# Seven GpSimd instructions fewer, and another order of VectorE's last products, in a state-space block with a gated FFN

## The chip, the cores and the metric

The kernel runs on one core of a Trainium2 chip. The metric is the device time of one execution in microseconds (us); a run gives one time and, for the core, its span in the profile's records. The time is usually 2.1 to 2.4 us longer than the span. In about one run of eight it is 2.8 to 3.9 us longer while the span is as usual, so spans are given beside times where tenths matter.

## The reference

Input x has 2048 tokens of 512 channels. It is normalised, then goes through two branches:

```python
xn = layernorm(x)
# branch A: a diagonal complex recurrence over the 2048 tokens
Bu = xn @ B_bar.T                       # complex, 512 states
h_t = Lam_bar * h_{t-1} + Bu_t
s = 2 * Re(h @ C.T) + xn * Dskip
# branch B: gated FFN with 1376 hidden columns, then silu
g = silu((gelu(xn @ w_gate) * (xn @ w_up)) @ w_down)
out = x + s * g
```

## The kernel before

The tokens are cut into four slabs (s = 0 to 3) of 512. TensorE does per slab: 11 pairs of products with w_gate and w_up (`g_ps`, `up_ps`, tile j), the input products of the recurrence (`u_ps`), the down projection (`f_ps`, four blocks of 11 matmuls) and the output product of the recurrence (`y_ps`). ScalarE applies gelu and copies (`gt`, `ub`). VectorE multiplies the two (`at`), rotates the states (`pp`, `qq`, `Wt`, `hst`), runs the scans (`Ft`) and multiplies and adds the outputs (`yg`, `ot`).

VectorE executes in program order, and the Python that writes the program decides that order with estimated clocks and a list of waiting work. An entry of the list is put in front of a new instruction when it would end by the time the new one is ready plus a tolerance `late`:

```python
def drain(t, late):
    while waiting and max(clk["dve"], waiting[0][0]) + waiting[0][1] <= t + late:
        pop()                                   # emits the head of the list

def dve(ready, cost, f, late=0.8):
    drain(ready, late)
    clk["dve"] = max(clk["dve"], ready) + cost
    f()                                         # emits the new instruction

def ffn(s, j, at):
    ...                                         # matmuls, gelu, copy
    if j == NFT - 1:                            # last tile, 96 rows
        dve(now() + lag, 0.36, lambda: TT(out=at[:fs, j, :], in0=gt[:fs, 0, :], in1=ub[:fs, 0, :], op=ALU.mult))
    elif i:                                     # two tiles at once
        dve(now() + lag, 0.63, lambda: TT(out=at[:, j - 1 : j + 1, :], in0=gt[:], in1=ub[:], op=ALU.mult))
```

The x of slab 3 is loaded late, since slab 0 keeps other data in its place until then; ScalarE takes its sums (`junk`), VectorE finishes the statistics (`ln_small`):

```python
def load_x(s):
    nc.sync.dma_start(out=x_tok[:, s * M : (s + 1) * M, :], in_=x_r[:, s * M : (s + 1) * M, :])
...
    if s == 1:
        load_x(3)
    for m in range(M):
        g2s[s, m] = down(s, m, ats[s])
        ...
        if s == 1:
            ln_act(3, m)
    if s == 1:
        ln_small(3)
```

## Time and profile before

| | before |
|---|---|
| times of the first three runs | 183.33, 183.81, 183.12 us |
| span in the profile | 181.0 us |
| TensorE busy | 96% of the span |
| VectorE busy | 89% |
| ScalarE busy | 62% |
| GpSimd busy | 12%, 49 instructions |

### The profile page before, as it was taken

What the parts mean: (1) busy time and instruction counts of PE and PEld (TensorE: products, weight loads), DVE (VectorE), ACT (ScalarE), POOL (GpSimd) and SP (SyncE); (2) the same over time, 40 slices, a digit from 0 to 9 for tenths busy, and PEclk for the clock granted to TensorE, in tenths of its full rate; (3) what the DMA queues carried; (4) which work ended last, traced back from release to release, by engine and by line L of the source; (5) the groups of instructions that cost most, each with busy time, mean ns of one, the idle gap of its engine ahead of it and who ended that gap; (6) DMA issues with size and microseconds to landing.
All of it is one profiled execution on the core that took longest, in us unless ns stands there. A gap on an engine that the chain in (4) does not pass through costs nothing.

```text
span 181.0 us, 2421 instructions
## 1 busy us (share of the span) xinstructions
PE 174.4 (96%) x842; PEld 82.9 (46%) x858; DVE 162.0 (89%) x256; ACT 112.4 (62%) x198; POOL 21.7 (12%) x49
## 2 busy tenths in 40 slices
PE   7899999999999999999999999999999999989992
PEld 2684444444444444444444444444444444444451
DVE  4789999997979999999958999999999999999163
ACT  3599766777699983681399953367239454563500
POOL 3795416004100000000004000000000000000000
PEclk9999999999999999999999999999999999999999
DMA  5999597961002300001300002510000000000011
GB/s 146 306 332 177 116 246 179 278 93 29 0 0 50 66 4 29 29 0 60 114 4 0 0 0 70 130 38 0 2 0 0 7 27 29 29 29 0 0 54 62
DMA packets 25644, 12.37 MB, mean 68 GB/s; under 512 B 15809, under 2 KB 25633, under 8 KB 25633
## 3 DMA queue, kind: packets, MB, share of 16 engines
q1 hardware_dynamic: 25456, 12.16, 28.3%
q8 instruction: 6, 0.10, 0.3%
q10 hardware_dynamic: 176, 0.07, 0.1%
q14 instruction: 6, 0.04, 0.1%
HBM read 6.46 MB, written 2.10 MB: 47 GB/s over the span
## 4 chain that ended last, share of the span: by engine, by line
DVE 44%; PE 42%; issue 5%; ACT 4%; DMA 3%; another core or an unknown queue 0%; SPq 0%; DVEq 0%; ACTq 0%
DVE Ft L432 12%; PE up_ps L243 10%; PE g_ps L243 10%; PE f_ps L493 9%; PE u_ps L385 8%; DVE qq L402 6%; DVE yg L526 5%; DVE pp L402 4%; PE y_ps L513 4%; DVE hst L406 4%; DMA x_tok<-in_A_x_dram 3%; DVE at L486 3%; DVE ot L527 3%; DVE Wt L406 3%; ACT junk L558 2%
## 5 line engine op out<-in xcount | busy, mean ns | idle before, releaser
L243 PE MATMUL g_ps<-xnT,wg 128*128 128x512 bf16 (+3 forms) x196 | 45.3, 353 | 0.5 <-DVE xnT L203 0.2
L243 PE MATMUL up_ps<-xnT,wu 128*128 128x512 bf16 (+3 forms) x188 | 45.2, 361 | 0.2
L493 PE MATMUL f_ps<-wd,at 128*128 128x512 bf16 (+1 forms) x172 | 38.7, 379 | 0.8 <-DVE at L484 0.6
L477 ACT ACTIVATE gt<-g_ps 128x512 bf16<-128x512 f32 (+1 forms) x44 | 27.1, 616 | 17.8 <-PE g_ps L243 16.1
L478 ACT ACTIVATE ub<-up_ps 128x512 bf16<-128x512 f32 (+1 forms) x44 | 27.0, 613 | 5.6 <-PE up_ps L243 5.0
L432 DVE TENSOR_TENSOR_SCAN Ft<-rho,it,Wt 128x512 bf16<-128x512 f32 x24 | 29.5, 1270 | 0.0
L385 PE MATMUL u_ps<-xnT,BT 128*128 128x512 bf16 x125 | 28.3, 379 | 0.2
L243 PEld LDWEIGHTS <-wg 128*128 128x128 bf16 (+1 forms) x200 | 19.1, 100 | 19.5 <-issue 0.5
L513 PE MATMUL y_ps<-C,hst 128*128 128x512 bf16 x119 | 27.6, 379 | 0.1
L243 PEld LDWEIGHTS <-wu 128*128 128x128 bf16 (+1 forms) x192 | 18.8, 100 | 19.1
L493 PEld LDWEIGHTS <-at 128*128 128x128 bf16 (+1 forms) x176 | 17.1, 98 | 21.7 <-DVE at L484 1.1
L390 ACT ACTIVATE U<-u_ps 128x512 bf16<-128x512 f32 x32 | 19.1, 597 | 9.8 <-PE u_ps L385 9.7
L498 ACT ACTIVATE g<-f_ps 128x512 f32<-128x512 f32 x16 | 9.5, 593 | 17.5 <-PE f_ps L493 17.5
L385 PEld LDWEIGHTS <-BT 128*128 128x128 bf16 x128 | 12.5, 98 | 15.1 <-DMA BT<-in_A_B_re_dram 0.2
L513 PEld LDWEIGHTS <-hst 128*128 128x128 bf16 x120 | 11.8, 98 | 14.1
L526 DVE TENSOR_TENSOR yg<-y_ps,g 128x512 bf16<-128x512 f32 x15 | 10.2, 682 | 5.8 <-PE y_ps L513 5.3
L486 DVE TENSOR_TENSOR at<-gt,ub 128x1024 bf16<-128x1024 bf16 x20 | 13.6, 679 | 0.0
L406 DVE TENSOR_TENSOR hst<-pp,qq 128x1024 bf16<-128x1024 bf16 x16 | 10.7, 688 | 0.3
L406 DVE TENSOR_TENSOR Wt<-pp,qq 128x1024 bf16<-128x1024 bf16 x16 | 10.4, 689 | 0.2
L402 DVE TENSOR_TENSOR pp<-U,cos_b 128x2048 bf16<-128x2048 bf16 x8 | 9.7, 1218 | 0.1
L402 DVE TENSOR_TENSOR pp<-Ft,cos_b 128x2048 bf16<-128x2048 bf16 x8 | 9.8, 1219 | 0.1
L402 DVE TENSOR_TENSOR qq<-U,sin_b 128x2048 bf16<-128x2048 bf16 x8 | 9.7, 1218 | 0.0
(116 smaller groups left out, 144.0 us busy)
## 6 DMA issues: line engine op xcount, KB each, us to landing
out_dram<-ot SPq DMA_DIRECT2D x15, 128.0 KB, 1.7
x_tok<-in_A_x_dram SPq DMA_DIRECT2D x3, 512.0 KB, 7.1
wd<-in_B_w_down_dram SPq DMA_DIRECT2D x1, 1280.0 KB
wg<-in_B_w_gate_dram SPq DMA_DIRECT2D x2, 256.0 KB, 4.3
wu<-in_B_w_up_dram SPq DMA_DIRECT2D x2, 256.0 KB
wg<-in_B_w_gate_dram SPq DMA_DIRECT2D x1, 512.0 KB, 6.5
wu<-in_B_w_up_dram SPq DMA_DIRECT2D x1, 512.0 KB
wg<-in_B_w_gate_dram SPq DMA_DIRECT2D x1, 352.0 KB
```

What stands on the lines that cost most here:

```text
L243: nc.tensor.matmul(ps[:fs, a:b], lhsT=w[:, kt, fsl], rhs=xnT[:, kt, s * TS + a : s * TS + b], start=(kt == 0), stop=(kt == KT - 1),)
L385: nc.tensor.matmul(u_ps[:, :], lhsT=BT[:, ri, kt, pt * P : (pt + 1) * P], rhs=xnT[:, kt, cols], start=(kt == 0), stop=(kt == KT - 1),)
L390: ACT(out=U[:, ri, q, :], in_=u_ps[:, :], func=AF.Copy)
L402: TT(out=box[key][:], in0=src()[:], in1=tab[:, hs, :].unsqueeze(1).to_broadcast(W), op=ALU.mult)
L406: return lambda: TT(out=dst()[i], in0=box["pp"][:, i, :, :], in1=box["qq"][:, 1 - i, :, :], op=op)
L432: nc.vector.tensor_tensor_scan(out=box["F"][:, ri, q, :], data0=rho[:, pt : pt + 1].to_broadcast([P, TS]), data1=box["W"][:, ri, q, :], in ...
L477: ACT(out=gt[:fs, i, :], in_=g_ps[:fs, :], func=AF.Gelu_apprx_tanh)
L478: ACT(out=ub[:fs, i, :], in_=u_ps[:fs, :], func=AF.Copy)
L486: dve(now() + lag, 0.63, lambda: TT(out=at[:, j - 1 : j + 1, :], in0=gt[:], in1=ub[:], op=ALU.mult))
L493: nc.tensor.matmul(f_ps[:, :], lhsT=at[:fs, k, m0 : m0 + P], rhs=wd[:fs, k, :], start=(k == 0), stop=(k == NFT - 1))
L513: nc.tensor.matmul(y_ps[:, :], lhsT=hst[:, j // NPT, j % NPT, m0 : m0 + P], rhs=C2[:, j // NPT, j % NPT, :], start=False, stop=(j == 2 * N ...
L526: TT(out=yg[:], in0=y_ps[:, :], in1=g2[:], op=ALU.mult)
```

## The change

The intent: take work off GpSimd (the identity is built in bf16 at once, three constants are set on VectorE, a factor 2 goes into a denominator, a bias that slab 1 does not use is not computed), move work into VectorE's waits, and put the last gate products of slab 3 ahead of waiting scans. The core of the diff (cuts marked):

```diff
-    ident_f = consts.tile([P, P], FP32, name="ident_f")
-    make_identity(nc, ident_f[:])
     ident = consts.tile([P, P], BF16, name="ident")
-    nc.gpsimd.tensor_copy(out=ident[:], in_=ident_f[:])
+    make_identity(nc, ident[:])
-    nc.gpsimd.memset(mhalf[:], -0.5)          # likewise eps, euler
+    nc.vector.memset(mhalf[:], -0.5)
...
+        GS(out=den[:], in0=den[:], scalar1=0.5, scalar2=None, op0=ALU.mult)
-        GS(out=cre[:], in0=cre[:], scalar1=2.0, scalar2=None, op0=ALU.mult)
-        GS(out=cim[:], in0=cim[:], scalar1=2.0, scalar2=None, op0=ALU.mult)
...
-        dve(now() + 0.8, 0.66, lambda: STT(   # fold_c, first half
+        dve(now() + 1.7, 0.7, lambda: STT(
-        dve(now() + 1.6, 0.66, lambda: STT(   # fold_c, second half
+        dve(now() + 2.4, 0.7, lambda: STT(
...
-            dve(now() + lag, 0.36, lambda: TT(...))
+            dve(now() + lag, 0.36, lambda: TT(...), 0.0 if s == NS - 1 else 0.8)
-            dve(now() + lag, 0.63, lambda: TT(...))
+            dve(now() + lag, 0.65, lambda: TT(...), 0.0 if s == NS - 1 and j > 8 else 0.8)
...
-        dve(now() + 1.0, 0.3, f)              # ln_small
+        dve(now() + 3.0, 0.3, f)
...
+        if x == 2:                            # nb only for slab 2
             G.tensor_tensor(out=nb[:, x, :], in0=mv[:, x, :, 0], in1=rs[:, x, :], op=ALU.mult)
             G.tensor_scalar(out=nb[:, x, :], in0=nb[:, x, :], scalar1=-1.0, scalar2=None, op0=ALU.mult)
```

More of the change, by code (lines that the diff above doesn't have):

```diff
@@ L140 @@
     eps = consts.tile([P, 1], FP32, name="eps")
-    nc.gpsimd.memset(eps[:], EPS)
+    nc.vector.memset(eps[:], EPS)
     sd = consts.tile([P, M], FP32, name="sd")
     euler = consts.tile([P, NPT], FP32, name="euler")
-    nc.gpsimd.memset(euler[:], math.e)
+    nc.vector.memset(euler[:], math.e)
     def small(name, w=NPT):
@@ L483, in ffn @@
         if j == NFT - 1:
-            dve(now() + lag, 0.36, lambda: TT(out=at[:fs, j, :], in0=gt[:fs, 0, :], in1=ub[:fs, 0, :], op=ALU.mult))
+            dve(
+                now() + lag, 0.36,
+                lambda: TT(out=at[:fs, j, :], in0=gt[:fs, 0, :], in1=ub[:fs, 0, :], op=ALU.mult),
+                0.0 if s == NS - 1 else 0.8,
+            )
         elif i:
-            dve(now() + lag, 0.63, lambda: TT(out=at[:, j - 1 : j + 1, :], in0=gt[:], in1=ub[:], op=ALU.mult))
+            dve(
+                now() + lag, 0.65, lambda: TT(out=at[:, j - 1 : j + 1, :], in0=gt[:], in1=ub[:], op=ALU.mult),
+                0.0 if s == NS - 1 and j > 8 else 0.8,
+            )
     def down(s, m, at):
@@ L623, in ln_vector_small @@
         G.tensor_tensor(out=rs[:, x, :], in0=vx[:, x, :], in1=mhalf[:], op=ALU.pow)
-        G.tensor_tensor(out=nb[:, x, :], in0=mv[:, x, :, 0], in1=rs[:, x, :], op=ALU.mult)
-        G.tensor_scalar(out=nb[:, x, :], in0=nb[:, x, :], scalar1=-1.0, scalar2=None, op0=ALU.mult)
+        if x == 2:
+            G.tensor_tensor(out=nb[:, x, :], in0=mv[:, x, :, 0], in1=rs[:, x, :], op=ALU.mult)
+            G.tensor_scalar(out=nb[:, x, :], in0=nb[:, x, :], scalar1=-1.0, scalar2=None, op0=ALU.mult)
     vx = consts.tile([P, NS, M], FP32, name="vx")
```

## The prediction

> **What bounds the kernel now.** I read the page first (busy shares, slices), then the waits of TensorE, then the VectorE and TensorE timelines, and last the neighbourhood of the one late wait.
>
> ```profile
> PE 174.4 (96%) x842; PEld 82.9 (46%) x858; DVE 162.0 (89%) x256; ACT 112.4 (62%) x198; POOL 21.7 (12%) x49
> PE f_ps L493 <- DVE at L484: 0.6, 1, 0.6
> PE tp L181 <- DVE xn L171: 0.2, 1, 0.2
> PE g_ps L243 <- DVE xnT L203: 0.2, 1, 0.2
> ```
>
> The first line gives busy us per engine, the others who TensorE (PE) waited for (total, times, longest). TensorE is busy for 96% of the span; after its first real matmul at 6.4 us it records one wait, 0.6 us, for the last gate product of slab 3 (line 484). GpSimd (POOL) is busy 12% and nowhere in that list. So the time is TensorE's stream plus a head and a tail, and only what shortens one of these three shows in the time.
>
> The late wait in the timeline (start, duration, engine, line, operation):
>
> ```profile
> 158.42 2.45 DVE L432 TENSOR_TENSOR_SCAN Ft<-rho,it,Wt 128x512 bf16<-128x512 f32 x2
> 160.37 0.59 ACT L478 ACTIVATE ub<-up_ps 96x512 bf16<-96x512 f32 x1 [0.33 <-PE up_ps L243]
> 160.79 0.67 DVE L486 TENSOR_TENSOR at<-gt,ub 128x1024 bf16<-128x1024 bf16 x1
> 161.38 1.28 DVE L432 TENSOR_TENSOR_SCAN Ft<-rho,it,Wt 128x512 bf16<-128x512 f32 x1
> 162.57 0.40 DVE L484 TENSOR_TENSOR at<-gt,ub 96x512 bf16<-96x512 bf16 x1
> ```
>
> VectorE runs a scan at 161.38 although the input of the last product was ready at 160.37 + 0.59 = 160.96. The product ends at 162.97, and TensorE resumes at 163.02. Three of the four down-projection blocks, and what follows the last one:
>
> ```profile
> 40.06 9.68 PE L493 MATMUL f_ps<-wd,at 128*128 128x512 bf16 x43
> 82.38 9.68 PE L493 MATMUL f_ps<-wd,at 128*128 128x512 bf16 x43
> 160.11 2.32 PE L493 MATMUL f_ps<-wd,at 128*128 128x512 bf16 x10
> 163.02 7.53 PE L493 MATMUL f_ps<-wd,at 96*128 96x512 bf16 x33 [0.59 <-DVE at L484]
> 170.39 5.13 PE L513 MATMUL y_ps<-C,hst 128*128 128x512 bf16 x23
> ```
>
> The next group after the first block starts at 49.57, after the second at 91.89: both 9.51 us from first matmul to next group (44 matmuls, 0.216 each). The last block takes 170.39 - 160.11 = 10.28. So the real loss is 10.28 - 9.51 = **0.77 us**; the 0.59 shown is less because the modelled end of a matmul overlaps the gap.
>
> **What the Trainium skill says.** "Perfetto Trace Analysis", Optimization Strategies: when the matmul engine is idle waiting for others, optimize the engines on the critical path. The trace agrees: all 21.7 us of GpSimd work leave no wait on TensorE. The same page, Tensor Engine Instruction, says ScalarE, VectorE and GpSimd are strict FIFO: an instruction put early in the list also blocks everything behind it. The trace agrees with the cost of that: VectorE stood still 1.82 us for the statistics at line 564. "SBUF — State Buffer", Who interferes with whom: a VectorE instruction with two SBUF inputs contends with GpSimd instructions that read SBUF. Here it is GpSimd that varies (the product of line 624 takes 0.20 us at 20.27 and 0.59 at 44.52), while VectorE's line 402 takes 1.20 and 1.22 beside busy GpSimd (26.4 to 28.7) and 1.22 without. So removing GpSimd work should give VectorE little.
>
> **Part 1, the start (identity, constants).** Removed on GpSimd: the cast of line 130, 0.29 us, and three memsets of 0.10. Identity is complete at about 1.64 and first used at 4.70, behind eight warm-up matmuls; eps is complete at 2.23 and first used at 4.51 behind the statistics. The head hangs on x landing at 2.80, then VectorE and ScalarE. The three memsets added to VectorE cost about 0.06 each (the one of line 126) in a gap from 1.12 to 2.80. **Effect 0.**
>
> **Part 2, coefficients and slab 1 and 2 statistics.** One halving of den is added (about 0.2 us, the tiny operations of lines 306 to 313), two doublings go (0.22 + 0.62), and two operations on nb for slab 1 go (0.20 + 0.24). The coefficient chain ends at 30.17 now and at about 29.3 then; it is first used at 43.1. The slab 1 norm needs rs, not nb. **Effect 0.**
>
> **Part 3, order on VectorE.** The kernel fixes this order with two clocks and a waiting list. I followed that rule on paper with old and new constants; with the old ones it gives the sequence in the timeline. Three groups move.
>
> - Folding of C (43 to 53 us). Two z products now fill part of the 1.06 us wait (0.7), and qq fills the 0.88 us wait before the last fold. Then the first gate product of slab 1, which needs ScalarE's ub at 54.16 + 0.62 = 54.78, makes VectorE wait some 0.6. Net VectorE gain about 0.35; TensorE sees none of it, as it has no wait there.
> - Slab 3 statistics (93 to 100 us). A pp of 1.14 (start to start) goes into the 1.82 us wait. But the product of slab 2, tiles 0 and 1, now precedes the second hst. It needs ub, done at 98.51 + 0.62 = 99.13, while VectorE would reach it at about 97.9. So the 1.14 gained is given back in a 1.2 us wait; hst would end near 100.4, where product after hst ended about 100.3 before: **0 to 0.15 later**, no gain. From here to 167.9 VectorE had no gap, so nothing else gives it time.
> - End of slab 3. New order: scan 0, products 8 and 9, product 10, scans 1, 2, 3. Step by step: scan 0 at 158.42 as before, products 8 and 9 at 159.65 (their ub was ready at 158.58 + 0.60 = 159.18), finished issuing at 160.25. Then VectorE waits, head of line, for ub at 160.96: about 0.75 us idle. Product 10 runs 161.02 to 161.42. TensorE reaches the eleventh matmul of the block at 160.11 + 10 x 0.216 = 162.27. Margin 0.8 us, so the wait is **gone, -0.77 us**.
>
> What the idle 0.75 costs: scan 1 at 161.34, scans 1.19 apart, pp 1.31 after the last one's start at 163.72, thus 165.03; qq 166.17; hst 167.42 to 168.71 instead of 167.88, 168.86 with the slab 2 delay. The y matmuls will start at 170.39 - 0.77 = 169.62, and their third is the first to need this half. Margin over 0.7. After that the tail is TensorE-paced (VectorE waits for y_ps 4.5, 0.57, 0.58 us), so it moves whole.
>
> Sum: 0 + 0 + 0 - 0.77. Span 181.00 - 0.77 = 180.23; time 183.33 - 0.77 = **182.56 us**, 0.4% less.
>
> **Rivals.** (a) The wait moves from at to hst: VectorE idles 0.75, and the last scan chain is 0.8 to 1.0 later. For it: VectorE has no gap between 96 and 167.9, so any delay travels to the end. Against it: before, hst was done 2.5 us ahead of the y matmuls. It needs a further delay of 0.8; then the gain shrinks from 0.77 to between 0 and 0.5: 182.8 to 183.3. (b) GpSimd matters for the head: the seven instructions shorten the start, or the freed read port speeds VectorE. For it: VectorE did wait 0.43 us for s2a at 10.82. Against it: that chain begins at 5.26, on pf from ScalarE, and none of its links is removed. At best 0.2 to 0.4 more: 182.2. (c) The earlier placement of gate products or y products makes VectorE late in slabs 1 to 3 until TensorE lacks a buffer or hst. Against it: checked at each moved y product, its matmuls are done before VectorE arrives (slab 3, block 1: 146.46 against 146.83, the closest). If it happened, 0.5 to 1 us: 183.3 to 184.
>
> **Range and chances.** The three runs before spread over 183.12 to 183.81, so a median moves by 0.2 to 0.3 on its own. Centre 182.6; rival (b) and luck give 182.2, rival (a) and ill luck 183.2. A change of 2% would be 3.7 us; the only stall that could be removed is 0.77, so faster by over 2% has 0.01. Slower by over 2% would take a stall that I missed several times over: 0.01. Within 2%: 0.98.
>
> **What would show it.** Right: TensorE's list of waits without line 484; last block 9.5 us long; a VectorE wait of about 0.7 us before the 96-row product, for ScalarE's ub; one of about 1.2 us before the first product of slab 2; hst ending near 168.7 and y starting near 169.6; GpSimd 42 instructions and some 20 us. Wrong: y_ps waiting for hst (a), the first g_ps matmul earlier than 6.42 by over 0.1 (b), or a new TensorE wait anywhere from 50 to 160 us (c).

## More of the kernel before

Read a busy share together with the waits: TensorE has almost no gap, so its stream is the time, plus what comes before and after it. The lines for this are in the prediction. One more view of the page belongs beside them, the chain of work that ended last, by engine (shares of the span):

```profile
DVE 44%; PE 42%; issue 5%; ACT 4%; DMA 3%; another core or an unknown queue 0%; SPq 0%; DVEq 0%; ACTq 0%
```

Followed back from the end, the chain leaves TensorE (PE) at the last gate product and spends more of the span on VectorE (DVE) than on TensorE, and it also holds transfers (DMA): the first load of x, 2.05 us, and the load of slab 3's x, 3.91 us.

## The result, and the profile after

The changed kernel took **182.59 us** (median of 6 runs, 182.53 to 183.06). The kernel before took 183.56 us (median of 6, 182.96 to 183.92). The ratio is 0.9956, 95% interval 0.9934 to 0.9979. Ratios here and below are the mean time of one kernel's fast runs over that of the other's of the same rounds, so not quite the ratio of the medians quoted. The prediction was 182.6, range 182.2 to 183.2. All outputs are right.

The page after, in busy us per engine, and the chain that ended last, by engine:

```profile
PE 175.2 (97%) x858; PEld 82.9 (46%) x858; DVE 161.8 (90%) x259; ACT 112.5 (62%) x198; POOL 20.4 (11%) x42
...
PE 94%; DVE 2%; DMA 1%; ACT 1%; issue 0%; DVEq 0%
```

GpSimd has 42 instructions instead of 49. The chain is now TensorE for 94% of the span. TensorE's list of waits has two entries left of four, neither for a gate product (the 1.2 us in front of the first warm-up matmul are there before too; the prediction shows the list from the first real work on):

```profile
PE w_ps L151 <- DVE euler L142: 1.2, 1, 1.2
PE g_ps L241 <- DVE xnT L201: 0.2, 1, 0.2
```

The end of slab 3 in the timeline:

```profile
158.28 1.28 DVE L429 TENSOR_TENSOR_SCAN Ft<-rho,it,Wt 128x512 bf16<-128x512 f32 x1
...
159.47 0.67 DVE L488 TENSOR_TENSOR at<-gt,ub 128x1024 bf16<-128x1024 bf16 x1
...
160.24 9.67 PE L497 MATMUL f_ps<-wd,at 128*128 128x512 bf16 x44
160.50 0.59 ACT L475 ACTIVATE ub<-up_ps 96x512 bf16<-96x512 f32 x1 [0.33 <-PE up_ps L241]
...
161.12 0.42 DVE L483 TENSOR_TENSOR at<-gt,ub 96x512 bf16<-96x512 bf16 x1 [0.98 <-ACT ub L475]
161.46 3.62 DVE L429 TENSOR_TENSOR_SCAN Ft<-rho,it,Wt 128x512 bf16<-128x512 f32 x3
...
167.52 1.29 DVE L403 TENSOR_TENSOR hst<-pp,qq 128x1024 bf16<-128x1024 bf16 x2
...
169.75 5.34 PE L517 MATMUL y_ps<-C,hst 128*128 128x512 bf16 x24
```

The last product runs at 161.12 instead of 162.57 and ends at 161.54. TensorE needs it at 160.24 + 10 x 0.216 = 162.40, so the 44 matmuls are one piece and y follows 9.51 us after their start. VectorE pays with 0.98 us of standing idle in front of the product, and the second half of hst ends at 168.81 instead of 167.88. That is still ahead of y.

To compare profiles whose starts differ, I cut TensorE's stream at two marks: the first u matmul (**u1**) and the first y matmul of slab 3 (**y**). In the changed kernel y - u1 is 169.75 - 17.73 = 152.02; before it was 170.39 - 17.61 = 152.78. From u1 to the last block's start it is 142.5 us in both, so all of the 0.76 lies in the last block. The head gave 0.12 us back (u1 at 17.73 against 17.61).

### The profile page after: what moved, and what is told of

Same layout as the page of the kernel before. It is cut to its first block, busy times and chain, and to the rows that moved or that the text cites. A ratio compares the mean times of both kernels' runs of the same rounds, so it can differ in the third digit from the quotient of the medians.

```text
span 180.4 us, 2432 instructions
## 1 busy us (share of the span) xinstructions
PE 175.2 (97%) x858; PEld 82.9 (46%) x858; DVE 161.8 (90%) x259; ACT 112.5 (62%) x198; POOL 20.4 (11%) x42
## 4 chain that ended last, share of the span: by engine, by line
PE 94%; DVE 2%; DMA 1%; ACT 1%; issue 0%; DVEq 0%
PE up_ps L241 21%; PE f_ps L497 21%; PE g_ps L241 21%; PE u_ps L382 15%; PE y_ps L517 14%; DMA x_tok<-in_A_x_dram 1%; DVE st L158 1%; PE tp L179 1%; DVE yg L549 0%; DVE yg L530 0%; ACT xnT L199 0%; DVE ot L550 0%; DVE xn L169 0%; ACT sd L164 0%; DVE mv L161 0%
## 5 line engine op out<-in xcount | busy, mean ns | idle before, releaser
L241 PE MATMUL g_ps<-xnT,wg 128*128 128x512 bf16 (+3 forms) x200 | 45.9, 353 | 0.3 <-DVE xnT L201 0.2
L241 PE MATMUL up_ps<-xnT,wu 128*128 128x512 bf16 (+3 forms) x192 | 45.7, 361 | 0.0
```

Of the source, the lines that this page charges most:

```text
L241: nc.tensor.matmul(ps[:fs, a:b], lhsT=w[:, kt, fsl], rhs=xnT[:, kt, s * TS + a : s * TS + b], start=(kt == 0), stop=(kt == KT - 1),)
```

## The experiments

There were twelve runs, of ten kernels (e9 and e10 repeat e2 and e3). "u1", "block" (start of the last down-projection block to y; 9.51 is without loss) and "y - u1" come from the one profile of each run of the table, the time from all executions. The kernel before was run beside each group on the same chip: e1 to e4 on one, e5 to e8, e9 and e10, e11 and e12 on three others. It was profiled only once, at the start.

| run | time, us | ratio to before (95%) | median span, us: this / before | u1 | block | y - u1 |
|---|---|---|---|---|---|---|
| before (first profile) | 183.33 | | | 17.61 | 10.28 | 152.78 |
| changed | 182.59 | 0.9956 (0.9934 to 0.9979) | 180.4 / not recorded | 17.73 | 9.51 | 152.02 |
| e1_end_only | 182.78 | 0.9964 (0.9949 to 0.9979) | 180.3 / 181.3 | 17.99 | 9.51 | 152.02 |
| e2_all_but_end | 182.90 | 0.9974 (0.9961 to 0.9986) | 180.7 / 181.3 | 17.52 | 10.12 | 152.62 |
| e3_gpsimd_only | 183.88 | 1.0036 (1.0006 to 1.0067) | 181.4 / 181.3 | 17.80 | 10.13 | 152.63 |
| e4_last_only | 182.93 | 0.9986 (0.9951 to 1.0022) | 180.7 / 181.3 | 18.10 | 9.52 | 152.02 |
| e5_late | 184.61 | 1.0053 (1.0009 to 1.0098) | 182.4 / 181.4 | 18.20 | 11.33 | 153.83 |
| e6_default_end | 182.51 | 0.9951 (0.9898 to 1.0004) | 180.4 / 181.4 | 17.78 | 9.51 | 152.01 |
| e7_dose1 | 182.58 | 0.9937 (0.9909 to 0.9965) | 180.4 / 181.4 | 18.18 | 9.52 | 152.02 |
| e8_dose4 | 187.38 | 1.0181 (1.0144 to 1.0219) | 185.2 / 181.4 | 18.03 | 9.51 | 152.01 |
| e9_all_but_end_again | 183.05 | 0.9995 (0.9977 to 1.0014) | 180.9 / 180.7 | 18.03 | 9.78 | 152.28 |
| e10_gpsimd_again | 183.05 | 1.0007 (0.9979 to 1.0036) | 180.9 / 180.7 | 17.75 | 9.78 | 152.28 |
| e11_split_x3 | 183.15 | 0.9986 (0.9953 to 1.0018) | 180.9 / 181.5 | 17.76 | 9.78 | 152.28 |
| e12_after_split_x3 | 182.62 | 0.9956 (0.9924 to 0.9989) | 180.5 / 181.5 | 17.52 | 9.52 | 152.01 |

### e1: the end of slab 3 alone

On the kernel before:

```diff
-            dve(now() + lag, 0.36, lambda: TT(...))
+            dve(now() + lag, 0.36, lambda: TT(...), 0.0 if s == NS - 1 else 0.8)
-            dve(now() + lag, 0.63, lambda: TT(...))
+            dve(now() + lag, 0.63, lambda: TT(...), 0.0 if s == NS - 1 and j > 8 else 0.8)
```

> The kernel before with nothing changed but the order at the end of slab 3 (last two gate products ahead of the remaining scans). Theory (only the lateness of the last gate product costs time): the whole gain, 0.7 to 0.9 us under the kernel before, the last down-projection block 9.5 us from first matmul to the next group, no TensorE wait for a gate product. GpSimd rival (the seven instructions shorten the head): at most half of the gain here, under 0.4 us. Rival of the middle (the two earlier reorderings give VectorE slack that is needed): the y matmuls wait for hst, gain under 0.4 us.

Measured: ratio 0.9964, the median 0.65 us under that of before (183.43), the block 9.51 us, no TensorE wait for a product. This one edit gives the whole gain to within the noise. The GpSimd part is not needed.

### e2: everything but the end of slab 3

The changed kernel with `late` 1.2 for the last pair and the last product of slab 3, which restores the old order at the end.

> The changed kernel with the end of slab 3 put back into the order of before (two scans, product pair, scan, last product, scan); all else of the change stays, GpSimd part and both reorderings in the middle. Theory: no gain, within 0.2 us of the kernel before, and the TensorE wait for the last gate product is back (0.5 to 0.8 us in the list of waits, the last block 10.2 to 10.4 us). GpSimd rival and rival of the middle: a gain of 0.4 us or more stays.

Measured: the wait is back, and the block is 10.12 us. But the kernel was 0.5 us faster than before, which the theory had not expected. The block explains 0.16 of that (10.28 - 10.12). The profile shows u1 at 17.52, with e12 the earliest of all. Left open here and taken up with e9.

### e3: the GpSimd part alone

The kernel before with the GpSimd edits of the diff (first two and last pieces above) and nothing else.

> The kernel before with only the GpSimd part of the change (identity in bf16, constants set on VectorE, factor 2 in the denominator, no nb for slab 1); VectorE's order of before otherwise. Theory: within 0.2 us of the kernel before; first real matmul within 0.1 us of 6.42; GpSimd busy about 20.4 us in 42 instructions; the wait for the last product stays at about 0.6. GpSimd rival: 0.2 to 0.4 us or more faster.

Measured: 0.45 us slower by the median, 0.1 us longer by the median span; the first real matmul at 6.30, GpSimd busy 20.6 us in 42 instructions, the block 10.13 us. The first real matmul is 0.12 us earlier, just past the 0.1 that the theory allowed, but this does not last: u1 is at 17.80, 0.19 later than before. No gain. That the median time is 0.45 longer comes in good part from runs with an unusual time beyond the span (185.31 us with a span of 181.4).

### e4: only the very last product moved

```diff
-            dve(now() + lag, 0.36, lambda: TT(...))
+            dve(now() + lag, 0.36, lambda: TT(...), 0.0 if s == NS - 1 else 0.8)
```

The pair keeps its old tolerance of 0.8.

> The kernel before with only the very last product moved, by one scan: two scans, product pair, last product, two scans. Theory: the last product would start at about 161.4, its input being there since 160.96, and end at about 161.8, ahead of the 162.27 at which TensorE needs it. So the whole gain of 0.7 to 0.9 us, and no idle time of VectorE before the last product, against 0.98 us in the changed kernel; hst would end near 167.9 as before. Rival (both products must go forward): the wait of TensorE stays in part, gain under 0.4 us.

Measured: the block is 9.52 us, and VectorE has no idle time before the product. In the timeline:

```profile
161.29 0.67 DVE L491 TENSOR_TENSOR at<-gt,ub 128x1024 bf16<-128x1024 bf16 x1
161.87 0.41 DVE L486 TENSOR_TENSOR at<-gt,ub 96x512 bf16<-96x512 bf16 x1
162.21 2.45 DVE L432 TENSOR_TENSOR_SCAN Ft<-rho,it,Wt 128x512 bf16<-128x512 f32 x2
```

The product follows its pair at once and ends at 162.28. TensorE needs it at 160.60 + 2.16 = 162.76. So one of the two moves is enough. Its time, 0.5 us under before by the medians and 0.6 by the spans, is less sharp (one of six runs had a span of 182.6, so the ratio's interval reaches 1.0022). u1 was late in this profile, at 18.10.

### e5: the last product moved the other way

`late` 2.4 for the last product, so that it follows the last scan.

> The kernel before with the last product moved the other way, behind the last scan. Theory: it would start at about 163.77 and end at 164.17, TensorE would go on at 164.22 instead of 162.27, so it loses 1.95 us instead of 0.77: 1.2 us slower than before (1.0 to 1.4), TensorE's wait about 1.8 us. If the lateness of this product were hidden or counted otherwise (rival: the tail is set by hst or by the output), under 0.4 us slower.

Measured: 0.9 us slower by the medians, 1.0 by the median spans, so just under and at the lower edge of what was expected (1.0 to 1.4). The block is 11.33 us, so the loss is 1.82 instead of 0.77. TensorE's list of waits has it (the profile's figure, 1.6, is again smaller than the loss):

```profile
PE f_ps L500 <- DVE at L486: 1.6, 1, 1.6
```

This excludes that the output or hst sets the tail: what the product is late by is what the kernel is longer by.

### e6: the changed kernel with the old tolerance

`late` back to 0.8 for both products, all else of the change kept.

> The changed kernel with the old constants (tolerance of 0.8 for all products) at the end of slab 3 but everything else of the change. The bookkeeping then gives: scan, product pair, scan, last product, two scans. Theory: the last product would end near 161.85 on the old time axis, ahead of the 162.27 at which it is needed, so the gain stays: 0.6 to 0.9 us under the kernel before, no TensorE wait for it. Rival (the zero tolerance is what gives the gain): within 0.3 us of the kernel before.

Measured: 182.51 us, block 9.51, no wait. The zero tolerance itself is not what gives the gain. With the other new constants the old tolerance also puts the last product early enough. What counts is the resulting order, not the number in the diff.

### e7 and e8: how much room the chain to hst has

After the last product of the changed kernel, one or four spare VectorE products into a dead part of `xnT`:

```diff
+            if s == NS - 1:
+                for _ in range(1):     # e8: range(4)
+                    TT(out=xnT[:, :, 0:TS], in0=cos_b[:], in1=sin_b[:], op=ALU.mult)
```

> The changed kernel with one spare VectorE product of 1.14 us after the last gate product (its output is not used). It measures what room the VectorE chain to hst has. Theory: in the changed kernel the second half of hst ends at 168.2 and 168.8, and the y matmuls that need it start at 170.2 and 171.0; so 1.14 us more fits: within 0.2 us of the changed kernel. Rival (the wait has moved to hst, which is now critical): 0.5 to 1.1 us slower than the changed kernel.

Measured: 182.58 us, y - u1 unchanged at 152.02. The rival "the wait moved to hst" falls: there is room for more than 1.1 us.

> The same with four spare products, 4.55 us. Theory: the room is about 2.0 us, so TensorE must wait for hst: 2.6 us slower than the changed kernel (2.2 to 3.0), that is 1.8 us slower than the kernel before, with a TensorE wait before the y matmuls of about 2.5 us. If VectorE's chain did not gate the y matmuls at all: no change.

Measured: 187.38 us, 4.8 us slower than the changed kernel, not 2.6. The direction is right, the size is not. TensorE's timeline:

```profile
170.04 0.60 PE L520 MATMUL y_ps<-C,hst 128*128 128x512 bf16 x2
173.47 6.61 PE L520 MATMUL y_ps<-C,hst 128*128 128x512 bf16 x22 [2.83 <-DVE hst L403]
179.92 1.91 PE L548 MATMUL y_ps<-C,hst 128*128 128x256 bf16 x16
```

The third y matmul should start at 170.04 + 2 x 0.216 = 170.47 and starts at 173.47: 3.00 us (the four products took 4.91 us, not 4.55, so the room was 1.91 us, near the expected 2.0). The other 22 take 179.92 - 173.47 = 6.45 instead of 22 x 0.216 = 4.75: another 1.70. The windows view (per stretch: busy us and count for the five engines, granted TensorE clock, DMA share, GB/s) tells why:

```profile
160.00:170.00 10.00, 10.00 (x48) 4.53 (x47) 8.80 (x9) 5.11 (x8) 0.00 (x0) 1.00 0.00 0
...
173.40:177.00 3.60, 3.53 (x9) 1.33 (x10) 1.31 (x3) 0.00 (x0) 0.00 (x0) 0.53 0.00 0
177.00:181.00 4.00, 4.00 (x25) 2.24 (x23) 2.32 (x5) 0.00 (x0) 0.00 (x0) 1.00 0.19 66
```

The granted clock was 0.53 on average over 3.6 us after the wait. The Trainium skill, "TensorE: Matmul & The Clock Gate", What's actually happening, describes this: a clock gate halves TensorE's clock after an idle window of about 3.4 us, and some 3.4 us of activity lifts it again. The trace agrees in kind. Sum: 3.00 + 1.70 = 4.70 us, and u1 of this profile was 0.30 later than in the changed kernel's: 5.0, against 185.3 - 180.4 = 4.9 in the spans.

### e9 and e10: e2 and e3 once more

> The kernel of e2_all_but_end once more, unchanged, because it came out 0.5 us faster than before although its wait was back. In its profile the last block lost 0.61 us, only 0.16 less than before, so 0.4 us must lie in the head. Theory (the head varies by some tenths from kernel to kernel and load to load, whatever the code): this time anywhere from 0.5 faster to 0.3 slower than before, last block 10.1 to 10.2 us, and 142.5 us from the first u matmul to the last block as in every profile. Rival (something in the code of this kernel shortens the head): again 0.4 to 0.6 us faster, first u matmul again near 17.5 us.

> The kernel of e3_gpsimd_only once more, unchanged; its head is the same code as that of the run beside it, and yet it came out 0.45 us slower than before. Theory: the head is variation, so this time from 0.5 faster to 0.5 slower than before, and the two kernels may change places. Rival (the GpSimd part lengthens the head, and something else in the other kernel makes up for it): again 0.3 to 0.6 us slower than before, first u matmul at 17.8 or later.

Measured, on another chip: both 183.05 us, ratios 0.9995 and 1.0007. The 0.5 faster and 0.45 slower of the first time are not properties of these kernels. That part of the theory held. But the blocks did not come out as expected: 9.78 in both, a loss of 0.27 us instead of 0.6, and e9 had the same program as e2, e10 the same as e3. **The loss is not a fixed property of the order.** My theory so far, "the order at the end costs 0.77", falls in its size.

What varies with it is a transfer. In the kernel before, the timeline of ScalarE and VectorE around 90 us and the issue of the load of slab 3's x:

```profile
84.81 0.39 SPq L101 DMA_DIRECT2D x_tok<-in_A_x_dram  x1
...
88.74 0.63 ACT L558 ACTIVATE junk<-x_tok 128x512 bf16<-128x512 bf16 x1 [3.19 <-DMA x_tok<-in_A_x_dram]
...
95.99 0.17 DVE L567 TENSOR_SCALAR sx<-sx 128x4 f32<-128x4 f32 x1
```

ScalarE waits 3.19 us for the load, takes 7.0 us for the sums, VectorE finishes them at 96 and then has no gap until the last product: 162.97 - 95.99 = 66.98 us. So the last product hangs on the landing of this load, while TensorE's need for it hangs on TensorE's own head. The landing relative to u1 and the loss (block - 9.51) in the profiles with the old order at the end:

| profile | first junk - u1 | loss |
|---|---|---|
| before | 71.13 | 0.77 |
| e3 | 70.99 | 0.62 |
| e10 | 70.51 | 0.27 |
| e2 (with the reorderings in the middle) | 71.23 | 0.61 |
| e9 (same program as e2) | 70.70 | 0.27 |

With the same order, a later landing goes with a larger loss. From e3 to before it is 0.14 later, and the loss is 0.15 larger. (With the reorderings in the middle VectorE needs less time from the landing to the first scan at the end, 69.42 us in e2 against 69.68 before, hence the smaller loss of e2.) The load itself took 3.93 us from issue to first use before (88.74 - 84.81) and 3.33 in e10 (88.26 - 84.93):

```profile
84.93 0.39 SPq L101 DMA_DIRECT2D x_tok<-in_A_x_dram  x1
...
88.26 0.63 ACT L555 ACTIVATE junk<-x_tok 128x512 bf16<-128x512 bf16 x1 [2.57 <-DMA x_tok<-in_A_x_dram]
```

Both short loads, 3.33 in e10 and 3.51 in e9, are from the chip of e9 and e10; the ten other profiles with one transfer have 3.79 to 4.04 (eight of them on two other chips). So it may be the chip rather than the single run; this was not tested. The issue comes at u1 + 67.2 in all profiles. And the kernels with the early last product were not merely lucky with their load: it landed at u1 + 71.15 in the changed kernel, 71.00 in e1 and 71.13 in e4, as late as in the profiles that lost 0.62 and 0.77, and they lost nothing.

### e11 and e12: the load of slab 3's x in four pieces

```diff
-        nc.sync.dma_start(out=x_tok[:, s * M : (s + 1) * M, :], in_=x_r[:, s * M : (s + 1) * M, :])
+        n = 1 if s == NS - 1 else M
+        for a in range(s * M, (s + 1) * M, n):
+            nc.sync.dma_start(out=x_tok[:, a : a + n, :], in_=x_r[:, a : a + n, :])
```

e11 is this on the kernel before, e12 on the changed one.

> The kernel before with VectorE's order untouched; only the load of slab 3's x (512 KB, one transfer, landing 3.3 to 3.9 us after its issue) is cut into four of 128 KB. Theory, as it stands after ten runs (in the kernel before, the last product hangs on a chain that starts with the landing of this load: load, ScalarE statistics 7.0 us, then VectorE without a gap for 67 us; TensorE waits only because that chain ends later than its own): the first statistics start 1.5 to 2 us earlier, at about 87 us, VectorE's chain with them, the last product ends by about 161.5, and TensorE's wait is gone. So the same gain as the change, 0.3 to 0.9 us against the kernel before, and y starts 152.0 us after the first u matmul. Rival (the lateness comes from the order of the scans as such, wherever the chain starts): the wait stays at 0.3 to 0.6 us, no gain.

Measured in e11: the first statistics start at 87.09 (u1 + 69.33, 1.8 earlier than before). The loss falls from 0.77 to 0.27 in the block, though not one VectorE instruction was moved. By the median spans on the same chip the kernel is 0.6 us shorter (180.9 against 181.5). By the times the ratio is 0.9986 and unclear, since two of the six runs had 3.3 us beyond their span. The theory wanted the loss gone, the rival wanted 0.3 to 0.6. 0.27 is just what e9 and e10 had, so something else takes over there. VectorE's timeline of e11 shows it:

```profile
157.01 0.69 DVE L528 TENSOR_TENSOR yg<-y_ps,g 128x512 bf16<-128x512 f32 x1 [0.65 <-PE y_ps L515]
157.73 0.42 DVE L529 TENSOR_TENSOR ot<-yg,x_tok 128x512 bf16<-128x512 bf16 x1
158.08 2.45 DVE L434 TENSOR_TENSOR_SCAN Ft<-rho,it,Wt 128x512 bf16<-128x512 f32 x2
160.45 0.67 DVE L488 TENSOR_TENSOR at<-gt,ub 128x1024 bf16<-128x1024 bf16 x1
161.03 1.27 DVE L434 TENSOR_TENSOR_SCAN Ft<-rho,it,Wt 128x512 bf16<-128x512 f32 x1
162.23 0.40 DVE L486 TENSOR_TENSOR at<-gt,ub 96x512 bf16<-96x512 bf16 x1
```

VectorE now has time and waits 0.65 us for TensorE's y product, at u1 + 139.25. In e9 and e10 the same instruction also starts at u1 + 139.25 and u1 + 139.24; before it was at 139.75, in e2 at 139.59. From there the old order leads to the end of the last product in 162.63 - 157.01 = 5.62 us, 0.2 us after TensorE's need at 160.26 + 2.16 = 162.42. So in these traces the old order loses 0.27 us even with an early load. A late landing adds up to 0.5 more.

> The changed kernel with the same cut of the load: does it beat both? Theory: no. TensorE has no wait left for VectorE, so an earlier VectorE is worth nothing: within 0.2 us of the changed kernel, 0.3 to 0.9 us under the kernel before; y again 152.0 us after the first u matmul. Rival (VectorE still holds the changed kernel up somewhere): faster than the changed kernel by 0.3 us or more.

Measured in e12: 182.62 us, ratio 0.9956, as the changed kernel's, y - u1 152.01. The cut load adds nothing to the changed kernel. I found no version faster than the changed kernel; e1, e6 and e12 equal the changed one.

## Why the prediction was right or wrong

- **Part 1 and part 2 (GpSimd), effect 0:** right. e3 and e10 show no gain, and e1 has the whole gain without them. GpSimd came out at 42 instructions and 20.4 us, as expected. The sign named for rival (b), a first g_ps matmul earlier than 6.42 by over 0.1, was just met in e3 and e10 (6.30 and 6.29; 6.36 in the changed kernel), but it did not reach u1 (17.80, 17.75 and 17.73 against 17.61). So rival (b) gave no time.
- **Part 3, folding of C:** right. The first wait shrank from 1.06 to 0.40 us, the wait before the first product of slab 1 appeared (0.59 us; 0.6 expected), and the scan behind it starts at 55.55 instead of 55.83. A wait of 0.63 us before the second fold, which the prediction did not name, came as well. TensorE saw none of it.
- **Part 3, statistics of slab 3:** right about the wait (1.16 us; 1.2 expected) and about hst (100.60 us; near 100.4 expected). Its conclusion "0 to 0.15 later" did not last to the end. VectorE reached scan 0 at 158.28, where before it was 158.42, though the load landed 0.14 later. Some 0.4 us came back between 138 and 155 us, in the new order of slab 3 (see the second point of the last section), though the prediction had said that nothing else gives VectorE time. The waits after this point were right in kind.
- **Part 3, end of slab 3, -0.77:** right in mechanism. The two timelines show it step by step: y - u1 fell by 0.76, product 10 ran from 161.12 to 161.54 (161.02 to 161.42 expected), hst ended at 168.81 (168.7 to 168.9 expected), y started at 169.75 (169.62 expected; the head was 0.12 later). The idle time before the product was 0.98, not 0.75, as VectorE came to it earlier and its input later (161.09 instead of 160.96). e1, e4 and e5 confirm the cause by doing the step alone, half of it and its opposite.
- **What the step missed:** it took 0.77 as the price of the order. The traces show 0.27, paid for the order even with an early load, plus up to 0.5 that depends on when slab 3's x lands, relative to TensorE's start. The prediction read the gapless VectorE from 96 us on, but did not ask what set its beginning. The chain view had the transfer in it. The sum came out right because the profile was one with a late landing, so in part by luck. By the spans of the kernel before such runs were the usual ones on three of the four chips of the experiments (median 181.3 to 181.5, against 180.7 on the fourth). No run of the changed kernel on that fourth chip is on record: what it is worth there stays open, and the loss of 0.27 in the two traces taken there suggests less.
- **Rival (a), hst:** rightly ranked. e7 shows over 1.1 us of room; e8 shows what happens when it is used up.
- **Rival (c), stalls in slabs 1 to 3:** none. u1 to the last block is 142.5 us in all fourteen profiles.
- **The skill on the shared port:** the argument that VectorE gains little from idle GpSimd was not tested by itself; e3 and e10 only agree with it.

## What to carry to other kernels

When an engine waits for a product of another, ask not only what stands in front of that product, but where the gapless stretch before it began: the lateness is the difference of two chains, and a transfer at the root of one can make it vary between runs of the same program, here between chips. To measure tenths of a microsecond, cut the trace at marks inside the busy engine's stream, so that the head's variation drops out (here 142.5 us between two marks in every profile, while the head moved by 0.7). And in a static order it can be enough to move the one instruction that the waiting engine needs; moving its neighbour too only made VectorE stand idle for 0.98 us.

## What the Trainium skill lacked or had wrong

- "TensorE: Matmul & The Clock Gate", What's actually happening: the table of states asks for an idle window of about 3.4 us (the page's closing table warns of gaps over about 3 us). Here a wait that the profile gives as 2.83 us (3.00 from expected to actual start) was enough for a mean granted clock of 0.53 over the next 3.6 us, at a cost of 1.70 us; a wait of 1.65 us (e5) was not, its clock stayed at 1.0.
- "VectorE: DVE Perf Modes", The DRAIN you can't avoid: a semaphore after each of eight tensor copies is measured there as free. Here an instruction that needs its predecessor's result starts about 0.12 us later than one that does not: qq to hst is 149.03 to 150.29 (1.26 us) before, qq to at is 149.14 to 150.28 (1.14) after; a scan to the pp that reads it is 145.52 to 146.83 (1.31) before, a scan to an unrelated yg 145.77 to 146.96 (1.19) after. Such pairs, broken up by the new order, are a likely source of the 0.4 us that VectorE won in slab 3; neither this nor the semaphore's part in it was tested by itself.
- No page says by how much one load varies between runs of the same program. Here a 512 KB load took 3.79 us from issue to first use in e3 and 3.33 in e10, 4.04 in e2 and 3.51 in e9, the same programs on two chips. Nor does one say that a run's time beyond its span can be 2.8 to 3.9 us instead of 2.1 to 2.4.
- "Perfetto Trace Analysis", Optimization Strategy, advises to look for the gaps on the engine in question. The loss of 0.27 us in e9, e10 and e11 is in no list of waits, since the modelled matmul ends cover it (the page itself calls a matmul's end an estimate); only the distance from start to start (9.78 against 9.51) shows it.
